# Rows of the DRAM tensor x with 528 instead of 521 columns in an attention-then-MoE kernel

## Chip, cores and metric

The kernel runs on one core of one Trainium2 chip. The time is the device time of one execution in microseconds (us). Three runs of the kernel before took 674.09, 674.44 and 675.66 us; their median is 674.44 us.

## What is computed

Chunked attention over 8 batches, 8 heads, 576 positions and 64 numbers per head (chunks of 64 positions), whose output, 4608 tokens of 512 numbers, goes through a mixture of 8 experts with one expert per token:

```python
x = attn_out.transpose(0, 2, 1, 3).reshape(B, S, H * D)      # 8 x 576 x 512
logits = einsum('bsd,de->bse', x, w_gate)                     # 8 experts
local_gate = sigmoid(einsum('bsd,de->bse', x, w_local))
for b in range(B):
    prev_e = -1
    for s in range(S):
        fresh_e = argmax(logits[b, s])
        e = fresh_e if (s == 0 or local_gate[b, s] < 0.5 or prev_e < 0) else prev_e
        prev_e = e
        p = softmax(logits[b, s])
        h = maximum(x[b, s] @ w1[e], 0)
        out[b, s] = p[e] * (h @ w2[e])
```

## The kernel before

The work is in two stages that overlap at their border.

**Attention** goes over 18 blocks of 256 tokens. For each, SP's queue loads `qt`, `kt` (line 131) and `v` (line 144); GpSimd (POOL) or another engine reorders q and k by heads into `qr` and `kr` (lines 162 and 164); TensorE (PE) transposes them (line 172) and ScalarE (ACT) copies the results out of PSUM; PE computes the scores `sc` (line 201); VectorE (DVE) takes the row maxima `mx` (line 212) and subtracts them (line 215); ACT takes the exponential (line 220); PE transposes the result and multiplies with v into `o` (line 250); DVE divides by the sums (lines 262 to 264) and so writes the block's 2 x 512 columns of x into the SBUF tile `xs` (three buffers). PE transposes `xs`, and `router` (from line 286) multiplies it with `wg9`, which holds per chunk of 128 features 32 columns: 8 of the router's weights, one of the local gate's, and 23 that a memset set to zero. The four chunks' results are transposed into `lg` (line 301), where each token then has 4 x 32 values. `red` (from line 305) adds the four chunks for the nine used columns into `L` (line 308), copies them beside x into columns 512 to 520 of `xs` (line 310), and SP writes the rows of `xs`, 521 numbers each, to `x_d` in DRAM (line 313, or line 316 for the two blocks that hold the last 64 tokens of four batches each).

**Routing** (`route`, from line 337) takes `L` on DVE in two halves of 18 columns of tokens, and makes of it the list of tokens of each expert. **The experts** go over tiles of 128 listed tokens: POOL gathers their rows from `x_d` (line 656, three tiles early into `raw`, 36 into `xg`), PE transposes them (line 650), they are split in a high and a low part (lines 652 and 653) and multiplied with `w1` (line 684) and `w2` (line 705) in three passes; the logits that came along in columns 512 to 519 give the probability (lines 668 to 675) by which DVE scales the result (line 1029), and POOL scatters it to the output (line 771).

The order of the work on PE, DVE, ACT and POOL around the change is written out by hand: `PAR["steady"]` gives it for one block in the middle of attention (`tp*8` the transposes of the exponentials, `s` the scores, `va` the products with v, `ra` the router, of which the first `ra*2` is the product and its copy, the second the transpose and `red`), and `PAR["drain"]` from the last blocks into the first expert tiles. SP's queue issues its transfers in program order, so a write to `x_d` that waits for DVE holds up the loads behind it.

Of the kernel before, what the change touches and what calls it, by code (L numbers as in the profile page):

```python
# [14 lines left out]
ALU = mybir.AluOpType  # L15
AX = mybir.AxisListType
# [5 lines left out]
E, F = 8, 1024  # L22
C = H * D
# [1 line left out]
P = 128  # L25
NT = N // P
NS = N // 256
XR = C + E + 1
HT = P // 2
DV = D + 2  # L30
TA = 18
# [36 lines left out]
def tile_attention_then_moe(ctx: ExitStack, tc, q, k, v, wg, wl, w1, w2, out):  # L68
    nc = tc.nc
# [4 lines left out]

    x_d = dpool.tile([N, XR], F32, name="x_d")

# [40 lines left out]
    def place(i):  # L117
        ph, j = divmod(i, 9)
        if j == LEFT:
            return 9 * ph + 8, [(4 * ph + n, 512, 64) for n in range(4)]  # L120
        j -= j > LEFT
        return 9 * ph + j, [(4 * ph + j // 2, 256 * (j % 2), 256)]
# [118 lines left out]
    def values(pT, vt, xs, fine=False):  # L241
        box = {}

        def group(j, h):
            if h == 0:
                box["o"] = ps_o.tile([P, 2, 512], F32, name="o")
            o = box["o"]
            for cp in range(2):
                for cc in range(2):
                    nc.tensor.matmul(  # L250
                        o[64 * cp:64 * cp + 64, cc, DV * h:DV * h + D + 1],
                        pT[64 * cc:64 * cc + 64, 4 * j + h, 64 * cp:64 * cp + 64],
                        vt[64 * cc:64 * cc + 64, cp, 4 * j + h, 0:D + 1],
                        start=True, stop=True,
                    )
            if h == 3 and not fine:
                norm(j)

        def norm(j):
                ov = box["o"][:, :, 0:4 * DV].rearrange("p c (h d) -> p c h d", d=DV)  # L260
                rs = pa2.tile([P, 2, 4], F32, name="rs")
                nc.vector.tensor_scalar_add(rs, ov[:, :, :, D], 1e-9)
                nc.vector.reciprocal(rs, rs)
                nc.vector.tensor_tensor(
                    xs[:, :, 256 * j:256 * j + 256].rearrange("p c (h d) -> p c h d", d=D),
                    ov[:, :, :, 0:D],
                    rs.unsqueeze(3).to_broadcast([P, 2, 4, D]),
                    ALU.mult,
                )

        out = []
        for j in range(2):
            out += [lambda j=j, h=h: group(j, h) for h in range(4)]
            if fine:
                out.append(lambda j=j: norm(j))
        return out
# [9 lines left out]
    def router(i, xT, xs, fine=False):  # L286
        lg = ps_l.tile([P, 2, 256], F32, name="lg")
        lT = pa2.tile([P, 256], F32, name="lT", bufs=1)

        def mm():  # L290
            for c in range(4):
                nc.tensor.matmul(lg[32 * c:32 * c + 32, 0], wg9[:, c], xT[:, c], start=True, stop=True)
            if not fine:
                cp()

        def cp():
            nc.vector.tensor_copy(lT, lg[:, 0])

        def tr():
            for cc in range(2):  # L300
                nc.tensor.transpose(lg[:, 1, P * cc:P * cc + P], lT[:, P * cc:P * cc + P], ident)
            if not fine:
                red()

        def red():
            slot, rows = place(i)
            Lt = L[:, 2 * slot:2 * slot + 2, :]
            nc.vector.tensor_reduce(
                Lt, lg[:, 1].rearrange("p (t c e) -> p t e c", t=2, c=4)[:, :, 0:9, :], AX.X, ALU.add)
            nc.vector.tensor_copy(xs[:, :, C:XR], Lt)  # L310
            if len(rows) == 1:
                (b, s0, n), = rows
                nc.sync.dma_start(x_d[S * b + s0:S * b + s0 + n, :].rearrange("(c p) n -> p c n", p=P), xs)
            else:
                for m, (b, s0, n) in enumerate(rows):
                    nc.sync.dma_start(x_d[S * b + s0:S * b + s0 + n, :], xs[64 * (m // 2):64 * (m // 2) + 64, m % 2])

        return [mm, cp, tr, red] if fine else [mm, tr]
# [157 lines left out]
    def a_va(i, fine=False):  # L476
        xss[i] = pa2.tile([P, 2, XR], F32, name="xs", bufs=3)
        return values(pTs.pop(i), vts.pop(i), xss[i], fine)
# [176 lines left out]
    def gather(t, dst, src):  # L655
        nc.gpsimd.indirect_dma_start(  # L656
            out=dst, out_offset=None, in_=src,
            in_offset=bass.IndirectOffsetOnAxis(ap=gidx[t].bitcast(U32), axis=0))
        return dst
# [122 lines left out]
    def early_gather():  # L782
        for t in range(EARLY):
            xgs[t] = gather(t, raw1[t][:, 0:XR], x_d[0:TA * P, :])

# [51 lines left out]
    for i in range(1, NS - 2):  # L837
# [10 lines left out]
        if 8 <= i < 16:  # L848
            c, col = divmod(i - 8, 2)
# [35 lines left out]
    def gather_full(t):  # L885
        xgs[t] = gather(t, pc.tile([P, XR], F32, name="xg", bufs=4), x_d)

# [226 lines left out]
```

## Time and profile before

| | |
|---|---|
| median of three runs | 674.44 us (674.09 to 675.66) |
| the profiled execution | 674.2 us |
| its span, first to last instruction | 672.4 us, so 1.8 us lie around it |
| mean granted TensorE clock | 0.985 of full speed |
| PE busy | 638.5 us, 95% of the span |
| DVE busy | 371.6 us, 55% |
| ACT busy | 271.6 us, 40% |
| POOL busy | 147.1 us, 22% |
| DMA | 97.38 MB, mean 145 GB/s |

Busy time is added up over all instructions of an engine. A share is a mean over stages that differ: attention and its drain fill about the first 190 us, the experts the rest. A wait is put down to the semaphore that came last; "issue" means that the engine waited for nothing that the profile shows.

### The profile page before, as it was taken

Reading aid. Unit: us, or ns where it says so; the run is one execution under the profiler, and the core shown is the slowest. Engines: PE = TensorE matmul, PEld = TensorE weight load, DVE = VectorE, ACT = ScalarE, POOL = GpSimd, SP = SyncE. Lnnn points to the kernel's source line nnn. Section 1 sums busy time; section 2 is a strip of 40 time slices with the busy share of each in tenths; the row PEclk is TensorE's granted clock in tenths of the full one; section 3 lists DMA queues with packets and bytes.
Section 4 is the critical chain, followed back from the end, with each engine's and each line's share of the span. In section 5 each row is a group of like instructions: output and inputs, shape, how many; then the busy total and the mean of one; then the engine's idle time right before and its main releaser. Section 6 shows DMA issues by size and latency. Waiting matters only on the chain. (4 is left out here: it accounts for less than half of the span.)

```text
span 672.4 us, 16746 instructions
## 1 busy us (share of the span) xinstructions
PE 638.5 (95%) x5552; PEld 509.7 (76%) x5552; DVE 371.6 (55%) x938; ACT 271.6 (40%) x434; POOL 147.1 (22%) x209
## 2 busy tenths in 40 slices
PE   4889998889999999999999999999999999999993
PEld 4778776777787888678888886788888888678882
DVE  2656666976783766664332455762377432476231
ACT  4567676655312143542212433531465222342220
POOL 5323353560051111121121121121113121112101
PEclk9899999999999999999999999999999999999997
DMA  9999999977521144235121254452167411144101
GB/s 252 265 263 267 262 268 278 263 221 235 194 100 76 34 158 158 92 110 177 35 64 34 65 175 135 160 153 66 34 212 265 148 45 55 33 160 172 53 19 35
DMA packets 102505, 97.38 MB, mean 145 GB/s; under 512 B 42257, under 2 KB 79121, under 8 KB 102353
## 3 DMA queue, kind: packets, MB, share of 16 engines
q1 hardware_dynamic: 96192, 75.69, 38.8%
q0 software_dynamic: 6160, 19.85, 8.9%
q8 instruction: 73, 1.20, 0.7%
q14 instruction: 80, 0.65, 0.3%
HBM read 76.48 MB, written 19.56 MB: 143 GB/s over the span
## 5 line engine op out<-in xcount | busy, mean ns | idle before, releaser
L705 PE MATMUL y<-w2h,hp 128*128 128x512 f32 x560 | 185.3, 401 | 1.6 <-ACTq L992 1.2
L684 PE MATMUL h<-w1h,xp 128*128 128x512 f32 x560 | 164.3, 403 | 0.0
L771 POOL DMA_INDIRECT out<-ysb,sidx x38 | 43.7, 1151 | 374.0 <-DVEq L976 269.9
L705 PEld LDWEIGHTS y<-w2h,hp 128*128 128x128 f32 x560 | 105.0, 188 | 26.2 <-issue 2.5
L684 PEld LDWEIGHTS h<-w1h,xp 128*128 128x128 f32 x560 | 102.5, 189 | 21.8
L705 PE MATMUL y<-w2l,hp 128*128 128x512 f32 x280 | 110.5, 395 | 0.0
L753 ACT ACTIVATE hsb<-h 128x1024 f32<-128x1024 f32 x35 | 35.9, 1027 | 161.5 <-PE h L684 149.0
L684 PE MATMUL h<-w1l,xp 128*128 128x512 f32 x280 | 88.2, 396 | 0.7 <-DVEq L970 0.7
L652 ACT CAST hp<-tr 128x512 fp32r<-128x512 f32 x76 | 41.2, 589 | 108.1 <-PE tr L650 100.6
L653 DVE TENSOR_TENSOR xp<-tr,xp 128x512 fp32r<-128x512 f32 x39 | 27.0, 691 | 88.2 <-ACTq L970 56.9
L684 PEld LDWEIGHTS h<-w1l,xp 128*128 128x128 f32 x280 | 52.5, 188 | 14.2 <-DVEq L970 1.1
L705 PEld LDWEIGHTS y<-w2l,hp 128*128 128x128 f32 x280 | 52.6, 188 | 11.1
L653 DVE TENSOR_TENSOR hp<-tr,hp 128x512 fp32r<-128x512 f32 x76 | 49.3, 686 | 13.5 <-ACT hp L652 5.7
L1029 DVE TENSOR_SCALAR ysb<-y,ppr 128x512 f32<-128x512 f32 x31 | 23.3, 751 | 32.4 <-PE y L705 31.5
L650 PE MATMUL tr<-ident,hsb 128*128 128x128 f32 x304 | 40.2, 273 | 0.3 <-ACT hsb L753 0.3
L650 PEld LDWEIGHTS tr<-ident,hsb 128*128 128x128 f32 x304 | 35.3, 140 | 6.8 <-ACT w2h L954 1.2
L656 POOL DMA_INDIRECT xg<-x_d,gidx x36 | 35.4, 983 | 21.6 <-issue 9.8
L960 DVE TENSOR_TENSOR w2l<-raw,w2h 128x1024 fp32r<-128x1024 f32 x28 | 33.1, 1223 | 6.5 <-DVEq L943 5.2
L960 DVE TENSOR_TENSOR w1l<-raw,w1h 128x1024 fp32r<-128x1024 f32 x28 | 32.4, 1221 | 6.0 <-ACT w1h L954 5.2
L212 DVE TENSOR_REDUCE mx<-sc 128x8 f32<-128x512 f32 x36 | 23.2, 685 | 20.4 <-PE sc L201 20.4
L954 ACT CAST w2h<-raw 128x1024 fp32r<-128x1024 f32 x28 | 28.6, 1048 | 12.4 <-PE y L711 5.4
L250 PE MATMUL o<-v,pT 64*64 64x65 f32 x1152 | 27.7, 230 | 3.5 <-issue 2.1
(198 smaller groups left out, 833.8 us busy)
## 6 DMA issues: line engine op xcount, KB each, us to landing
raw<-in_moe_w SPq DMA_DIRECT2D x72, 512.0 KB, 4.4
x_d<-xs SPq DMA_DIRECT2D x16, 521.0 KB, 6.2
v<-in_v SPq DMA_DIRECT2D x32, 256.0 KB, 6.4
qt<-in_q SPq DMA_DIRECT2D x15, 512.0 KB, 5.9
kt<-in_k SPq DMA_DIRECT2D x15, 512.0 KB, 6.5
x_d<-xs SPq DMA_DIRECT2D x8, 130.2 KB, 4.2
qt<-in_q SPq DMA_DIRECT2D x8, 128.0 KB, 5.6
kt<-in_k SPq DMA_DIRECT2D x8, 128.0 KB, 4.9
```

The lines of the kernel that those rows point to most:

```text
L250: nc.tensor.matmul(o[64 * cp:64 * cp + 64, cc, DV * h:DV * h + D + 1], pT[64 * cc:64 * cc + 64, 4 * j + h, 64 * cp:64 * cp + 64], vt[64 * ...
L650: nc.tensor.transpose(ps[:, n], src_of(n), ident)
L652: return [tr, lambda: nc.scalar.copy(hi, box["ps"]), lambda: V.tensor_tensor(lo, box["ps"], hi.bitcast(F32), ALU.subtract)]
L653: lambda: V.tensor_tensor(lo, box["ps"], hi.bitcast(F32), ALU.subtract)]
L656: nc.gpsimd.indirect_dma_start(out=dst, out_offset=None, in_=src, in_offset=bass.IndirectOffsetOnAxis(ap=gidx[t].bitcast(U32), axis=0))
L684: nc.tensor.matmul(hs[:, j], xs[a][:, c], W1[w][c][:, 512 * j:512 * j + 512], start=(c == 0 and n == 0), stop=(c == 3 and n == 2))
L705: nc.tensor.matmul(y, hx[f // 4][a][:, f % 4], W2[w][c][:, f % 2, :], start=(f == 0 and n == 0), stop=(f == 7 and n == 2))
L753: nc.scalar.activation(hsb, hs.rearrange("p j f -> p (j f)"), AF.Relu)
L771: nc.gpsimd.indirect_dma_start(out=out, out_offset=bass.IndirectOffsetOnAxis(ap=sidx[t].bitcast(U32), axis=0), in_=ysb, in_offset=None, bo ...
L954: nc.scalar.copy(hi[c], raw[c])
L960: V.tensor_tensor(lo[c], raw[c], hi[c].bitcast(F32), ALU.subtract)
L1029: V.tensor_scalar(ysb, y, pr, None, ALU.mult)
```

## The change

A row of `x_d` and of `xs` gets 528 columns, which is 2112 instead of 2084 bytes, a multiple of 64. `red` now adds the four chunks for 16 columns, the nine used ones and seven of the empty ones, straight into `xs`, and then copies the nine used ones from `xs` to `L`. The write to `x_d` and the gathers move the longer rows.

```diff
-XR = C + E + 1
+XR = C + 16
...
             nc.vector.tensor_reduce(
-                Lt, lg[:, 1].rearrange("p (t c e) -> p t e c", t=2, c=4)[:, :, 0:9, :], AX.X, ALU.add)
-            nc.vector.tensor_copy(xs[:, :, C:XR], Lt)
+                xs[:, :, C:XR], lg[:, 1].rearrange("p (t c e) -> p t e c", t=2, c=4)[:, :, 0:XR - C, :], AX.X, ALU.add)
+            nc.vector.tensor_copy(Lt, xs[:, :, C:C + E + 1])
```

PE and ACT have the same instructions in the same order as before. On DVE the two instructions of `red` are exchanged in what they write. The place in the middle of attention, with the normalisation of a block ahead and the maxima of the next scores behind:

```order
 L263 RECIPROCAL rs<-rs 128x8
 L264 TENSOR_TENSOR xs<-o,rs 128x2x256
-L308 TENSOR_REDUCE L<-lg 128x18
-L310 COPY xs<-L 128x2x9
+L308 TENSOR_REDUCE xs<-lg 128x2x16
+L310 COPY L<-xs 128x18
 L212 TENSOR_REDUCE mx_752<-sc 128x8
 L212 TENSOR_REDUCE mx_754<-sc 128x8
```

The write of `xs` to `x_d` now needs only the first of the two, while `L` comes with the second. The last block, on DVE, with the router's copy `lT` and the splitting of an early expert tile (`xp`, `hp`) around it and the second half of the routing (line 345) behind it:

```order
 L297 COPY lT<-lg 128x256
 L653 TENSOR_TENSOR xp<-tr,xp 128x512
-L308 TENSOR_REDUCE L<-lg 128x18
-L310 COPY xs<-L 128x2x9
+L308 TENSOR_REDUCE xs<-lg 128x2x16
+L310 COPY L<-xs 128x18
 L653 TENSOR_TENSOR hp_3320<-tr,hp_3320 128x512
 L345 TENSOR_REDUCE mxb<-L 128x18
```

Here the routing reads `L` one instruction after the pair, as before.

## Rows read from the trace of the kernel before

**Rows 1.** The page: the span, and busy time of PE.

```profile
span 672.4 us, 16746 instructions
...
PE 638.5 (95%) x5552; PEld 509.7 (76%) x5552; DVE 371.6 (55%) x938; ACT 271.6 (40%) x434; POOL 147.1 (22%) x209
```

**Rows 2.** Stretches of 20 us: busy us of each engine (instructions), clock, DMA share, GB/s.

```profile
40.00:60.00 20.00, 18.14 (x360) 14.64 (x361) 11.81 (x31) 12.12 (x20) 5.52 (x10) 0.91 1.01 263
...
120.00:140.00 20.00, 18.23 (x413) 14.57 (x412) 18.10 (x59) 13.50 (x23) 12.61 (x19) 0.91 0.81 207
...
320.00:340.00 20.00, 20.00 (x98) 16.39 (x97) 6.81 (x19) 3.87 (x7) 3.96 (x4) 1.00 0.18 54
```

**Rows 3.** PE in order of time: start, us, instructions [idle before, releaser].

```profile
47.16 0.47 PE L201 MATMUL sc<-kT,qT 64*64 64x64 f32 x17 [1.86 <-issue]
...
72.44 0.57 PE L201 MATMUL sc<-kT,qT 64*64 64x64 f32 x22 [1.58 <-issue]
...
100.97 1.09 PE L172 MATMUL tr<-ident,pr 128*128 128x128 f32 x8 [0.50 <-issue]
...
107.85 0.59 PE L292 MATMUL lg<-xT,wg 128*32 128x256 f32 x2 [1.46 <-issue]
...
132.23 0.21 PE L250 MATMUL o<-v,pT 64*64 64x65 f32 x1 [1.77 <-issue]
```

**Rows 4.** DMA queues from 69.6 to 72.5 us: packets, MB, share.

```profile
q1 hardware_dynamic: 2450, 0.77, 114.6%
q8 instruction: 1, 0.02, 2.1%
```

**Rows 5.** Two short stretches at half clock, columns as in rows 2.

```profile
47.60:51.10 3.50, 3.50 (x47) 3.05 (x44) 2.85 (x6) 1.17 (x2) 0.00 (x0) 0.51 0.95 216
133.00:136.40 3.40, 3.40 (x21) 2.17 (x19) 3.31 (x11) 1.58 (x3) 3.40 (x7) 0.50 0.10 32
```

**Rows 6.** Groups on DVE: out<-in, sizes, count | busy us, mean ns | idle before.

```profile
L672 DVE TENSOR_REDUCE psm<-pex 128x2 f32<-128x16 f32 x38 | 6.4, 169 | 1.2
...
L308 DVE TENSOR_REDUCE L<-lg 128x18 f32<-128x72 f32 x18 | 4.0, 223 | 0.2 <-PE lg L301 0.2
...
L310 DVE COPY xs<-L 128x18 f32<-128x18 f32 x18 | 3.4, 188 | 0.6
...
L881 DVE TENSOR_REDUCE qs<-q 128x36 f32<-128x288 f32 x1 | 0.7, 689 | 0.0
...
L353 DVE TENSOR_REDUCE mxb<-t 128x18 f32<-128x144 f32 x2 | 0.6, 304 | 0.0
```

**Rows 7.** DVE in order of time around three of the eighteen reductions, columns as in rows 3.

```profile
62.42 0.22 DVE L308 TENSOR_REDUCE L<-lg 128x18 f32<-128x72 f32 x1
...
63.68 1.29 DVE L212 TENSOR_REDUCE mx<-sc 128x8 f32<-128x512 f32 x2 [0.83 <-PE sc L201]
...
121.53 1.29 DVE L212 TENSOR_REDUCE mx<-sc 128x8 f32<-128x512 f32 x2 [0.25 <-PE sc L201]
...
137.34 0.17 DVE L262 TENSOR_SCALAR rs<-o 128x8 f32<-128x8 f32 x1 [0.97 <-PE o L250]
...
177.98 0.28 DVE L368 TENSOR_TENSOR_SCAN sc<-aT,zrow 18x64 f32<-18x64 f32 x1 [0.25 <-ACT aT L362]
```

**Rows 8.** DMA issues from 30 to 146 us: count, KB each, median us to landing.

```profile
x_d<-xs SPq DMA_DIRECT2D x12, 521.0 KB, 6.4
qt<-in_q SPq DMA_DIRECT2D x10, 512.0 KB, 6.8
...
raw<-in_moe_w SPq DMA_DIRECT2D x6, 512.0 KB, 6.0
```

**Rows 9.** DMA issues from 146 to 176 us.

```profile
raw<-in_moe_w SPq DMA_DIRECT2D x7, 512.0 KB, 5.2
x_d<-xs SPq DMA_DIRECT2D x4, 521.0 KB, 5.2
```

**Rows 10.** What SP's queue waited for: us in total, times, longest.

```profile
SPq L313 <- DVE xs L310: 5.9, 6, 2.1
```

**Rows 11.** PE at the first gathered tile that routing had to wait for.

```profile
200.53 0.40 PE L705 MATMUL y<-w2h,hp 128*128 128x512 f32 x1
200.76 0.60 PE L650 MATMUL tr<-ident,xg 128*128 128x128 f32 x4
```

## Prediction

> **What bounds the kernel now.** I read the busy times first, then the stretches of 20 us, then the gaps of PE in order of time. PE is busy for 638.5 of 672.4 us [rows 1]. In the experts' stage it leaves nothing: 20.00 of 20 us at full clock, with DMA at 0.18 of its capacity [rows 2]. What moves data faster gains nothing there. In attention PE is busy for 18.14 and 18.23 us of a stretch, and there the DMA engines are full (1.01, 263 GB/s) [rows 2]; that is the only stage where the change can be felt.
>
> What is PE waiting for there? Five gaps between 40 and 140 us stand in [rows 3], together 1.86 + 1.58 + 0.50 + 1.46 + 1.77 = 7.2 us. None waits for a load or for DVE; all are "issue", and three break a run of equal matmuls before its end (17 are left of one, 22 of another, one of a third), where nothing new is waited for. In the stretch of the second gap one 0.02 MB transfer of instructions runs beside data transfers of 114.6% of the engines [rows 4]. I take these gaps for PE waiting for its instructions, which come through the same full DMA engines; that reading is inferred. [...]
>
> **The change part by part.**
>
> *The reduction on DVE.* Line 308 reads 4 x 16 instead of 4 x 9 values for each of two tokens, 128 instead of 72. It takes 223 ns now [rows 6]. The trace has no reduction of 128 values that reads in strides in PSUM, so I bound it. Two that read in a row, 16 values in 169 ns and 144 in 304 ns [rows 6], give (304 - 169) / 128 = 1.05 ns per value; the one that reads in strides, 288 in 689 ns [rows 6], gives with the first (689 - 169) / 272 = 1.91. For 56 more values that is 59 to 107 ns each, and for 18 blocks 1.1 to 1.9 us of DVE. I take the lower end, because at 1.05 the present 72 values come to 169 + 56 x 1.05 = 228 ns, nearly the 223 measured, and at 1.91 to 276. So 18 x 59 = 1.1 us. The copy of line 310 has 18 values before and after: 188 ns, no change.
>
> What hides it: behind a reduction in mid-attention DVE soon waits for PE again. After the one at 62.42 us the maxima wait 0.83 us for the scores, and the shortest of these waits, at 121.53 us, is 0.25 us, still more than 0.107 [rows 7]. From there to 137.34 us DVE has no such pause; the one reduction at its start is covered by the 0.25 us, the next (128 us) by the 0.97 us at 137.34. PE's gap in that stretch isn't a wait for DVE [rows 3]. In the drain the last reduction is on the way to the second routing, and 0.25 us at 177.98 us cover it [rows 7]. Cost on the path: 0. Were that cover gone everywhere, it would be 1.1 us, at most 1.9.
>
> *The order of the pair.* The write to x_d needs one DVE instruction less ahead of it. Six times SP waits for line 310 [rows 10]; the write can go 188 - 59 = 129 ns earlier there, and the loads behind it too. L comes later by the 59 ns counted above. Nothing on PE waits for SP's loads in [rows 3], so the gain is 0.
>
> *Longer rows.* 521 KB become 528, 1.34%. At 263 GB/s [rows 2] such a write fills the DMA engines for 521 x 1.024 / 263 = 2.03 us, so 27 ns more each, and for 18 blocks 0.5 us of transfer in stretches where no gap of PE waits for data: 0 on the path. A gather of 128 rows grows by 3.6 KB, 14 ns at that rate. The first gather of the second routing is the only one near PE: its transposes follow the matmul before them without idle time [rows 11], so 14 ns might show there, once. The others run in a stage with DMA at 0.18.
>
> *Row starts.* Each row now starts at a multiple of 64 bytes from the first. What a ragged start costs isn't in the trace by itself. Bounds: between 146 and 176 us the writes of 521 KB land in 5.2 us, weight loads of 512 KB in 5.2 too [rows 9], so the ragged rows cost nothing. In the full stretch they take 6.4 us against 6.0 for weight loads and 6.8 for q [rows 8]: at the most 0.4 us of landing in each of 12, 4.8 us that nobody on PE waits for. I take 0, by the nearer row: [rows 8] has writes between the two kinds of loads. A loss isn't excluded either, and is the case of other gaps below.
>
> [...]
>
> **Sum.** 0 + 0 + 0 + 0 against the profiled execution's 674.2 us (span 672.4 and 1.8 around it), which is 0.2 us below the median of the runs. Forecast: 674.2 us, no change. About 0.2% (1.3 us) is what a measurement of this kernel can tell from no change.
>
> **Rivals.**
>
> *A, faster: the DMA engines get lighter and PE's instructions come in time.* If ragged rows do load the engines, the transfers of instructions beside them wait less, and gaps of [rows 3] go. For it: the engines are full in just those stretches [rows 2, 4]. Against it: the landing times of [rows 8, 9]. With the first gap and its stretch at half clock gone, 1.86 + 1.7 = 3.5 us: 670.7 us. All five gaps and both stretches would be 7.2 + 3.4 = 10.6 us, to 663.6; I don't believe that x_d alone causes them, as its writes are a fifth of the traffic from 30 to 146 us (12 x 0.533 MB [rows 8] of 263 GB/s x 116 us = 30.5 MB).
>
> *B, slower: one more such gap.* The write goes out some 0.13 us earlier and lasts 27 ns longer, so that another transfer of instructions comes behind it on a full engine. Place: the runs of 64 score matmuls or 32 products with v between 20 and 146 us, the work in which PE goes through its instructions fastest. It decides as soon as the instructions arrive after PE has used up those it has, and not before. Price: the four long gaps have a mean of (1.86 + 1.58 + 1.46 + 1.77) / 4 = 1.67 us, and a stretch at half clock may follow, 1.7 us: 675.9 to 677.6, middle 676.7 us. For it: the gaps are irregular, five in a dozen blocks of equal work, so their condition is nearly met elsewhere. Against it: the three runs shown lie within 1.6 us.
>
> *C, slower: DVE's longer reductions are exposed* in the drain and around 121 to 137 us, where DVE is busy 18.10 of 20 us [rows 2]: 1.1 to 1.9 us, 675.3 to 676.1 us.
>
> *D, the change doesn't do what it says:* the rows' first byte in DRAM isn't at a multiple of 64, so that all rows stay ragged. Then only the 1.34% and the reduction are left: 674.2 us, not to be told from the forecast by the time.
>
> **How the numbers follow.** Forecast with D 0.50; A 0.28, since full engines in the stage with gaps are the one real lever; B 0.16; C 0.06, half of it under 0.2%, but I count it as slower. So faster 0.28, same 0.50, slower 0.22. The range goes from A's 670.7 to B's 676.7: it leaves out A's larger and B's upper end, together under 0.2.
>
> **What would show it.** Right: line 308 at about 282 ns, 18 times, line 310 unchanged; PE's busy time and its five gaps as before; 20.00 of 20 us in the experts' stage; x_d landing at about 6.4 us in the full stretch. Wrong towards A: fewer or shorter "issue" gaps between 40 and 140 us, x_d landing clearly under 6.0, mean clock over 0.985. Wrong towards B: a sixth gap and another stretch at half clock. Wrong towards C: PE idle for DVE after 120 us. A change in the experts' stage would contradict the whole reading.

## The result, and the profile after

The changed kernel is slower: 677.21 us (median of 17 runs, 674.61 to 681.5) against 673.5 us for the kernel before on the same chip (17 runs, 669.61 to 676.02). The ratio is 1.0067, with a 95% interval of 1.0048 to 1.0085. The forecast was 674.2 us and no change; the range ended at 676.7.

The page of the changed kernel, its first lines:

```profile
span 677.0 us, 16746 instructions
...
PE 638.5 (94%) x5552; PEld 509.9 (75%) x5552; DVE 373.0 (55%) x938; ACT 271.6 (40%) x434; POOL 146.7 (22%) x209
```

PE is busy for the same 638.5 us as in [rows 1]; the span is 4.6 us longer. All that was added is standing still. The stretches of 20 us say where (columns as in [rows 2]):

```profile
40.00:60.00 20.00, 18.63 (x397) 14.90 (x397) 13.51 (x33) 13.57 (x24) 6.11 (x11) 1.00 1.11 269
...
80.00:100.00 20.00, 17.02 (x350) 13.79 (x348) 11.47 (x29) 12.25 (x22) 6.10 (x10) 0.91 1.07 229
...
120.00:140.00 20.00, 19.29 (x408) 15.42 (x406) 18.92 (x58) 14.83 (x26) 10.51 (x16) 1.00 1.03 253
...
320.00:340.00 20.00, 20.00 (x96) 16.27 (x95) 5.44 (x17) 4.50 (x8) 1.98 (x2) 1.00 0.12 39
```

The experts' stage is as full as it was, and the stretches from 40 and 120 us are even fuller than in [rows 2]. The loss lies in others, most of all from 80 to 100 us. The same stretch of the kernel before:

```profile
80.00:100.00 20.00, 19.85 (x453) 16.06 (x444) 14.11 (x34) 15.67 (x27) 8.82 (x13) 1.00 1.05 264
```

PE was busy for 19.85 us there, and now for 17.02, while the DMA engines are as full (1.07 after 1.05) and move 229 instead of 264 GB/s. PE in order of time shows what it stands for (columns as in [rows 3]):

```profile
40.87 0.68 PE L250 MATMUL o<-v,pT 64*64 64x65 f32 x28 [0.53 <-DMA v<-in_v]
...
90.43 0.43 PE L250 MATMUL o<-v,pT 64*64 64x65 f32 x4 [2.60 <-DMA v<-in_v]
...
100.49 0.68 PE L250 MATMUL o<-v,pT 64*64 64x65 f32 x28 [0.49 <-DMA v<-in_v]
...
110.27 0.68 PE L250 MATMUL o<-v,pT 64*64 64x65 f32 x28 [1.47 <-DMA v<-in_v]
...
206.20 0.60 PE L650 MATMUL tr<-ident,xg 128*128 128x128 f32 x4
```

Before, no gap of PE was a wait for a load. Now PE waits for v, seven times. What PE waited for, in total over the span (us, times, longest), with its waits for `xs` beside it:

```profile
PE o L250 <- DMA v<-in_v: 6.4, 7, 2.6
PE o L250 <- DVE xs L264: 3.6, 3, 2.2
```

The waits for `xs` in the kernel before:

```profile
PE o L250 <- DVE xs L264: 1.4, 2, 1.1
```

The "issue" gaps between 40 and 140 us went the other way, from 7.2 us in five [rows 3] to 2.2 us in three:

```profile
PE sc L201 <- issue: 1.2, 2, 0.8
PE o L250 <- issue: 1.0, 1, 1.0
```

So the 4.6 us are a balance of several waits, and not the waits for v alone.

The first gathered tile reaches PE at 206.20 us instead of 200.76 [rows 11], 5.4 us later: the loss is complete before the experts' stage. From that tile to the end of the span it takes 470.6 to 471.6 us in all fourteen profiled executions of this document, so every difference between their spans arises before it.

Stretches at half clock exist after the change too, at other places than in [rows 5]: the granted clock was at 0.50 after PE had stood still for 2.60 and for 1.47 us. Its mean over the span is 0.988, before 0.985, so the clock doesn't make the difference (columns as in [rows 2]):

```profile
90.50:93.90 3.40, 3.02 (x40) 2.68 (x40) 1.06 (x3) 0.40 (x1) 0.00 (x0) 0.50 1.04 228
111.00:114.40 3.40, 3.40 (x20) 2.19 (x21) 1.49 (x4) 1.28 (x3) 1.16 (x2) 0.50 1.20 303
```

The two instructions that were edited, in the groups on DVE:

```profile
L308 DVE TENSOR_REDUCE xs<-lg 128x32 f32<-128x128 f32 x18 | 5.0, 280 | 0.1
L310 DVE COPY L<-xs 128x18 f32<-128x18 f32 x18 | 3.2, 180 | 0.6
```

The reduction takes 280 ns; 282 were forecast. The landings from 30 to 146 us:

```profile
x_d<-xs SPq DMA_DIRECT2D x12, 528.0 KB, 6.8
v<-in_v SPq DMA_DIRECT2D x24, 256.0 KB, 7.0
qt<-in_q SPq DMA_DIRECT2D x11, 512.0 KB, 5.6
kt<-in_k SPq DMA_DIRECT2D x11, 512.0 KB, 7.0
raw<-in_moe_w SPq DMA_DIRECT2D x6, 512.0 KB, 5.5
```

Of the kernel before, the lines on v and k that [rows 8] leaves out:

```profile
v<-in_v SPq DMA_DIRECT2D x26, 256.0 KB, 6.4
kt<-in_k SPq DMA_DIRECT2D x10, 512.0 KB, 6.5
```

x_d lands in 6.8 us instead of 6.4, v and k in 7.0 instead of 6.4 and 6.5, q and weights even sooner than before [rows 8]. Landing times point at no one transfer. The decisive view is another one: the first 30 us, in which nothing is written to x_d yet (the first write is issued at 39.1 us before and at 42.6 us after). The DMA queue of SP there (packets, MB, and the time that the packets took as a share of the 16 engines, which can exceed 100%), of the kernel before:

```profile
q1 hardware_dynamic: 18444, 7.68, 103.2%
```

and of the changed kernel:

```profile
q1 hardware_dynamic: 16241, 6.57, 103.2%
```

The engines are equally full, and 14% less arrives. What slows the loads is there before the first long row is written, so the writing of the rows can't be it.

What else did the edit move? The constant `XR` is also the width of the SBUF tile `xs`, which has three buffers. In the compiled programs' tables of tiles the three xs tiles lie 4192 bytes apart before (2 x 521 x 4 = 4168 are used) and 4224 after (2 x 528 x 4 = 4224). The pools on that side of SBUF are stacked downwards there, so the lowest of them (at 186784, then at 186688) and every tile below it start 3 x 32 = 96 bytes lower, the destinations of the q and k loads among them; those of v and of the weights stay in place. From the same tables, the start of the first of three `qt` tiles in a partition (all tiles of qt and kt are 4096 bytes apart, so all have the same remainder):

| kernel | qt starts at | modulo 256 |
|---|---|---|
| before | 124416 | 0 |
| changed | 124320 | 160 |

The theories for the experiments are these. **S**: the q and k loads are slower because their tiles no longer start at a multiple of some power of two. **W**: the longer rows of x_d load the memory. **V**: the longer reduction on DVE. The expectations quoted below speak of them by these letters. Medians differ between the chips on which these runs were made (the kernel before took 668.02 to 673.5 us on them), so only ratios to the kernel before on the same chip are compared.

### The profile page after: what moved, and what is told of

It reads as the page before. It is cut to its first block, busy times and chain, and to the rows that moved or that the text cites. A ratio compares the mean times of both kernels' runs of the same rounds, so it can differ in the third digit from the quotient of the medians.

```text
span 677.0 us, 16746 instructions
## 1 busy us (share of the span) xinstructions
PE 638.5 (94%) x5552; PEld 509.9 (75%) x5552; DVE 373.0 (55%) x938; ACT 271.6 (40%) x434; POOL 146.7 (22%) x209
## 5 line engine op out<-in xcount | busy, mean ns | idle before, releaser
L250 PE MATMUL o<-v,pT 64*64 64x65 f32 x1152 | 29.1, 230 | 11.5 <-DMA v<-in_v 6.4
L250 PEld LDWEIGHTS o<-v,pT 64*64 64x64 f32 x1152 | 22.7, 138 | 19.7 <-DMA v<-in_v 8.0
```

The source lines that it names most:

```text
L250: nc.tensor.matmul(o[64 * cp:64 * cp + 64, cc, DV * h:DV * h + D + 1], pT[64 * cc:64 * cc + 64, 4 * j + h, 64 * cp:64 * cp + 64], vt[64 * ...
```

## The experiments

All that move qt and kt alone have the same edit, with another number (8 numbers are 32 bytes): an unused tile behind kt in the same pool, by whose size qt and kt move down while all other tiles stay.

```diff
         kt = pe2.tile([P, H, 2 * D], F32, name="kt", tag="kt", bufs=3)
+        if i == 0:
+            pe2.tile([P, 8], F32, name="gap", bufs=1)
```

**e1: The kernel before, qt and kt 32 bytes lower.**

> The kernel before, with 32 unused bytes behind kt in the pool of the loads, so that only the SBUF tiles qt and kt start 32 bytes lower: at 32 modulo 64, as in the changed kernel, instead of at a multiple of 64. Theory S (the change slowed the q and k loads by moving their SBUF tiles off multiples of 64 bytes): slower by 0.4 to 0.9%, about 677 us, PE idle for v loads between 40 and 140 us, less data moved in the first 30 us (under 235 GB/s against 257). Theory W (the longer x_d rows load the memory) and theory V (the longer reduction on DVE): within 0.2% of before.

Measured: ratio 1.0095 (1.0068 to 1.0123). An unused tile of 32 bytes makes the kernel before at least as slow as the change did. The first 30 us of SP's queue, and PE's waits for v:

```profile
q1 hardware_dynamic: 16155, 6.52, 101.6%
```

```profile
PE o L252 <- DMA v<-in_v: 6.5, 9, 1.9
```

This is the picture of the changed kernel, without any of its edits (the two added lines shift line 250 to 252). In the program's table of tiles nothing but qt and kt has moved, so it is their place that costs the time.

**e2: The changed kernel, qt and kt back at a multiple of 64.**

> The changed kernel with 32 unused bytes behind kt, so that qt and kt start at a multiple of 64 bytes again (not at one of 512 as before). Theory S: as fast as before or up to 0.4% faster, 670 to 674 us. A variant of S in which 512 bytes count: as slow as the changed kernel, about 677 us. Theories W and V: 677 us.

Measured: 1.0052 (1.0029 to 1.0076). Still slow; a multiple of 64 isn't enough (this one is at 128 modulo 256). The first 30 us:

```profile
q1 hardware_dynamic: 16836, 6.86, 102.5%
```

**e3: The changed kernel, qt and kt back at multiples of 512.**

> The changed kernel with 416 unused bytes behind kt, so that qt and kt start at multiples of 512 bytes as before. Theory S in both variants: as fast as before or up to 0.4% faster, 670 to 674 us. Theories W and V: 677 us.

Measured: 0.9974 (0.995 to 0.9998). The whole loss is gone with all seven columns still there, so W and V fall. The first 30 us:

```profile
q1 hardware_dynamic: 18013, 7.46, 99.0%
```

The first gathered tile reaches PE 9.0 us sooner here (first line) than in e1 (second), which ran on the same chip:

```profile
192.98 0.60 PE L652 MATMUL tr<-ident,xg 128*128 128x128 f32 x4
201.98 0.60 PE L652 MATMUL tr<-ident,xg 128*128 128x128 f32 x4
```

**e4: The kernel before, qt and kt 64 bytes lower.**

> The kernel before with 64 unused bytes behind kt: qt and kt move, but stay at multiples of 64 bytes. Theory S: within 0.2% of before. The variant with 512 bytes, and a theory that any move of these tiles costs time: slower by 0.4 to 0.9%, about 677 us. Theories W and V: within 0.2% of before.

Measured: 1.0114 (1.0079 to 1.015). I had taken 64 bytes for the unit; that was a miss. Moving by 64 costs as much as moving by 32. The first 30 us:

```profile
q1 hardware_dynamic: 16566, 6.73, 104.0%
```

This left two readings: a unit above 64, or a loss by any move of these tiles.

**e5: The kernel before, qt and kt 256 bytes lower.**

> The kernel before with 256 unused bytes behind kt: qt and kt start at 256 modulo 512. Theory S with 256 bytes as the unit that counts: within 0.3% of before, q and k pieces at the mean of before. Theory S with 512 bytes as the unit: slower by 0.5 to 1.1%, as with 32 and 64 bytes. A theory that any move of these tiles costs time (for instance by another alignment than the tiles behind them): slower by 0.5 to 1.1%.

Measured: 1.0009 (0.9986 to 1.0032). A move by itself costs nothing, and 256 bytes are enough. The first 30 us:

```profile
q1 hardware_dynamic: 17801, 7.35, 98.3%
```

**e12: The kernel before, qt and kt 128 bytes lower.**

> The kernel before with 128 unused bytes behind kt: qt and kt start at 128 modulo 256. Theory S with 256 bytes as the unit: slower than before by 0.4 to 1.1%; if the loss is the same at every place off the unit, 0.9 to 1.1% as with 32 and 64 bytes, if half the unit costs less, 0.4 to 0.8%, as e2 hints (0.52% slower with the rest of the change in it). A unit of 128 bytes: within 0.2% of before.

Measured: 1.0089 (1.0057 to 1.0121). 128 bytes are not enough, and they cost as much as 32 or 64. The first 30 us:

```profile
q1 hardware_dynamic: 16646, 6.77, 103.5%
```

The eight kernels side by side (aligned are those with qt at a multiple of 256); MB per full engine time is the MB of the first 30 us divided by the share, from the rows above, of one execution each:

| qt modulo 256 | kernel | ratio to before | MB at 100% |
|---|---|---|---|
| 0 | before | 1 | 7.44 |
| 0 | e5, before | 1.0009 | 7.48 |
| 0 | e3, changed | 0.9974 | 7.54 |
| 128 | e12, before | 1.0089 | 6.54 |
| 128 | e2, changed | 1.0052 | 6.69 |
| 192 | e4, before | 1.0114 | 6.47 |
| 224 | e1, before | 1.0095 | 6.42 |
| 160 | changed | 1.0067 | 6.37 |

The six kernels that follow all have qt at 0 modulo 256. They come to 7.5 to 7.6 MB, and e10 to 8.1, so no aligned kernel overlaps with one that isn't.

The next runs ask whether anything else in the change moves the time, and whether v, too, can be helped.

**e6: The kernel before, v rows 80 instead of 66 numbers apart.**

```diff
-DV = D + 2
+DV = D + 16
```

> The kernel before with the v tiles' rows of 64 numbers 80 numbers apart instead of 66 (320 bytes instead of 264), so that in one of the two v tiles all pieces start at multiples of 64 bytes and two of eight at multiples of 256; qt and kt stay in place. If the place of a piece modulo 256 is what counts (theory S): the v loads get lighter, before or faster, 0.1 to 0.5%. If only q and k matter: within 0.2% of before.

Measured: 0.9992 (0.9968 to 1.0016). No gain that can be told, where theory S for v forecast 0.1 to 0.5%. Either two aligned pieces of eight, in one of the two v tiles, are too few, or the place of v's pieces of 256 bytes matters less. That stays open: a pitch that puts all eight at multiples of 256 was not tried.

**e7: The changed kernel, qt and kt at multiples of 512, v rows 80 apart.**

> The changed kernel with qt and kt at multiples of 512 bytes (as in e3) and v rows 80 numbers apart (as in e6): the gains of both add up, 0.2 to 0.7% faster than before. Theories W and V: slower than before by 0.4 to 0.9%.

Measured: 0.9956 (0.9927 to 0.9984). The fastest ratio of all, and faster than both kernels; with e6 showing nothing, I don't put the difference to e3 down to v.

**e8: The kernel before, the pair of red exchanged alone.**

```diff
             nc.vector.tensor_reduce(
-                Lt, lg[:, 1].rearrange("p (t c e) -> p t e c", t=2, c=4)[:, :, 0:9, :], AX.X, ALU.add)
-            nc.vector.tensor_copy(xs[:, :, C:XR], Lt)
+                xs[:, :, C:XR], lg[:, 1].rearrange("p (t c e) -> p t e c", t=2, c=4)[:, :, 0:9, :], AX.X, ALU.add)
+            nc.vector.tensor_copy(Lt, xs[:, :, C:XR])
```

> The kernel before with the pair of red exchanged alone: the reduction of nine columns goes straight into xs and the copy makes L, rows stay at 521 columns, no tile moves. If the write to x_d, issued one DVE instruction earlier, is what makes the changed kernel with qt and kt at multiples of 512 a little faster than before: 0.1 to 0.4% faster. Theory S alone: within 0.2% of before.

Measured: 1.0015 (0.9993 to 1.0037). The earlier write gains nothing.

**e9: The kernel before with all SBUF tiles where e3 has them.** The tile xs gets 14 numbers that nobody uses, and 416 bytes lie behind kt.

```diff
-        xss[i] = pa2.tile([P, 2, XR], F32, name="xs", bufs=3)
+        xss[i] = pa2.tile([P, 2 * XR + 14], F32, name="xs", bufs=3)[:, 0:2 * XR].rearrange("p (c n) -> p c n", c=2)
```

> The kernel before with rows of 521 columns, but xs tiles of 4224 bytes and 416 unused bytes behind kt, so that all SBUF tiles lie where they lie in e3. If the places of the other tiles (xs as the source of the writes, xT, pr, pT) make e3 faster than before: 0.1 to 0.4% faster. If it is the rows of x_d, which start at multiples of 64 bytes in DRAM: within 0.2% of before. Theory S holds in both, since qt and kt are at multiples of 512.

Measured: 1.0007 (0.9981 to 1.0032). The places of the other tiles make no difference.

**e10: The changed kernel, qt and kt at multiples of 512, both v tiles at multiples of 256.**

```diff
-    vbuf = [pa1.tile([P, 2, H, DV], F32, name=f"v{i}") for i in range(NV)]
+    vbuf = [pa1.tile([P, n], F32, name=f"v{i}")[:, 0:2 * H * DV].rearrange("p (t h d) -> p t h d", t=2, h=H)
+            for i, n in enumerate((1408, 1392))]
```

(besides, `DV = D + 16`, and 160 unused bytes behind kt)

> The changed kernel with qt and kt at multiples of 512 bytes, v rows 80 numbers apart and both v tiles starting at multiples of 256 bytes, so that two of eight v pieces in each lie on a multiple of 256: as e7 or up to 0.2% faster, 0.3 to 0.7% faster than before.

Measured: 0.998 (0.996 to 1.0). Not better than e7 or e3. The first 30 us:

```profile
q1 hardware_dynamic: 17354, 7.13, 88.4%
```

That is 8.1 MB per full engine time, the most of all fourteen executions, in the one kernel with both v tiles at multiples of 256. So v's places may count for the engines too, by one execution; the kernel isn't faster for it.

**e11: The kernel of e3 once more.**

> The kernel of e3 once more, beside e8 and e9: 0.1 to 0.4% faster than before if the gain of e3 was more than the spread of the runs, within 0.1% if not.

Measured: 0.9984 (0.9957 to 1.001). Together with e3 (0.9974) the change itself, with its side effect taken away, comes out between no change and a gain of some 0.2%. The other runs point the same way: the aligned kernels with the long rows lie at 0.9956 to 0.9984 (e3, e7, e10, e11), those without at 0.9992 to 1.0015 (e5, e6, e8, e9); off the multiples it is 1.0052 and 1.0067 with them (e2, the changed kernel) and 1.0089 to 1.0114 without (e1, e4, e12). So some 0.2 to 0.4% of gain seem to lie under the loss. Neither the exchanged pair alone (e8) nor the places alone (e9) give it. The rows in DRAM, by their start or their length, are what is left as its cause; no run separates these, and none shows at which address x_d starts.

## Why the prediction was wrong

- **The step that failed** is the one on longer rows. It counted what the constant `XR` does to the transfers (27 ns for a write, 14 ns for a gather) and not what it does to the tile `xs` in SBUF. The sum "0 + 0 + 0 + 0" lacked a term: the q and k loads, which no line of the diff names, onto tiles 96 bytes lower. That term alone measured 0.9 to 1.1% of the time in the kernel before (e1, e4, e12); with the rest of the change it came to 0.7%. The order of the instructions holds no addresses; the program's table of tiles shows the move.
- **"None waits for a load"** was true of [rows 3] and was read as slack. With the engines at 1.01 of their capacity [rows 2] there was none to count on: when 14% less arrives, PE waits for v seven times, 6.4 us in all, although v's own tiles had not moved. I read that as v sharing queue and engines with q and k; no run shows it by itself. In the aligned kernels these waits are 0 to 5.2 us (5.2 in e8, which is no slower), in the others 5.3 to 6.6 us, so a wait for v doesn't tell by itself where the loss comes from. The ratio and the first 30 us do.
- **The five "issue" gaps** were taken for a property of the kernel, and two rivals and the signs of being wrong hung on them. That they are waits for instructions, no run shows. They belong to that one execution: e8, with the same places and rows, has none between 40 and 140 us. The changed kernel has fewer of them and a mean clock over 0.985, two of the three signs given for a gain, and is slower. Also, the engines are full only in the first of the two stretches quoted from [rows 2]; the second, with the last gap in it, is at 0.81.
- **A wait for DVE was missed.** "None waits for DVE" left out a gap of PE in the same 100 us, behind one of the reductions. It is 0.83 or 0.84 us in all eight runs with the reduction of nine columns and 0.89 in all six with sixteen, so the longer reduction does show on PE, once, by 0.05 us. And the 0.25 us at 177.98 us, counted as cover, is a wait for `aT`, which is itself made from `L`, so it covers nothing. Both are far too small to make the loss. The gap in the kernel before, then in the changed one:

```profile
112.34 0.49 PE L376 MATMUL tr<-ident,sc 18*1 18x18 f32 x4 [0.84 <-DVE sc L369]
118.08 0.49 PE L376 MATMUL tr<-ident,sc 18*1 18x18 f32 x4 [0.89 <-DVE sc L369]
```

- **Places were weighed in DRAM alone**, at the starts of the rows of x_d, and not in SBUF, where the loads land. There the runs show 256 bytes as the unit: 32, 64 and 128 bytes off it cost about the same (1.0095, 1.0114, 1.0089), 256 costs nothing (1.0009). What makes it the unit, no run here shows.
- **Rival A**, which I gave 0.28, had the engines as the lever in attention, which is right, and the wrong sign, since I saw only the x_d writes on them. The little gain that seems to lie under the loss (e11) would have A's sign; whether it has A's cause is not shown. **Rival B** forecast 676.7 us, near the measured 677.2, by luck, for its reason doesn't hold: the "issue" gaps of [rows 3] shrank, and waits for v were added.
- **The 1.7 us that both rivals count for a stretch at half clock** are shown by no run: none was made with such a stretch alone taken away. What the trace before shows is the time of the same work: eight transposes took 1.93 us in the stretch at 0.51 [rows 5], and eight of the same size 1.09 us soon after, where the clock is at 1.00 (52 to 56 us). The changed kernel has two such stretches as well, at 0.50, and is slower all the same. In the kernel before:

```profile
47.56 1.93 PE L172 MATMUL tr<-ident,xs 128*128 128x128 f32 x8
...
52.34 1.09 PE L172 MATMUL tr<-ident,kr 128*128 128x128 f32 x8
```

- **What held:** the reduction (280 ns, forecast 282) and its cover but for 0.05 us; the earlier write without effect (e8); the experts' stage at 20.00 of 20 us; and no change, or a little gain, once the tiles are back in place (e3, e11).

## What to carry to other kernels

A constant that sizes a tile can move the tiles placed behind it, here by 96 bytes: before costing such an edit, compare the places of all DMA destinations in the two programs, and hold those of a full DMA stage at multiples of 256 bytes, with a filler tile if need be. This is shown here for loads in pieces of 512 bytes (0.9974 and 0.9984 with the q and k tiles of the changed kernel at such multiples, 1.0067 without). The weight tiles, loaded in pieces of 2 and 4 KB, start at 192 modulo 256 in all these kernels, and moving them was not tried. This DMA stage, at 1.01 of its capacity [rows 2], had no slack to read off: that nobody waited for a load in [rows 3] said nothing about what 14% less would do (waits for v of 6.4 us). Where a transfer got slower, look at a stretch in which the suspected part hasn't begun yet.

## What was not expected

With the pieces of 512 bytes of q and k at 128, 160, 192 or 224 modulo 256 in SBUF, the queue moves 6.4 to 6.7 MB per full engine time of the first 30 us; with them at a multiple of 256 it moves 7.4 to 7.6, or 8.1 with v's tiles at multiples as well (e10). It is a step, not a slope: 32 bytes off a multiple cost as much as 128 (1.0095 and 1.0089). And 32 unused bytes in SBUF cost the kernel before 0.95% of its time.
